# RetNet retention with a leaky-ReLU feed-forward layer: the copy that begins a product's PSUM bank moved ahead of four activations, and a new order of banks and sums between the kernel's two parts

## The chip, the cores and the metric

The kernel runs on one core of a Trainium2 chip. The metric is the device time of the whole kernel in microseconds. The core's engines work side by side, each through its own queue of instructions: TensorE (PE) multiplies matrices into PSUM, an accumulator memory of 8 banks of 128 x 512 float32; VectorE (DVE) and ScalarE (ACT) read and write PSUM and the on-chip memory SBUF; GpSimd (POOL) works on SBUF; SyncE (SP) issues transfers (DMA).

## What is computed

The first part is a recurrent retention over 4 batches, 8 heads, 768 tokens and 64 dimensions, the second a feed-forward layer with a leaky ReLU over the 3072 tokens that result, with d_model 512 and d_ff 2048.

```python
for t in range(S):
    state = gamma * state + einsum('bhd,bhe->bhde', k[:, :, t], v[:, :, t])
    y[:, :, t] = scale * einsum('bhd,bhde->bhe', q[:, :, t], state)
x = y.transpose(0, 2, 1, 3).reshape(3072, 512)
h = x @ w_in
g = np.maximum(0.01 * h, h)
out = g @ w_out
```

## The kernel before

The tokens are cut into six chunks of C = 128 per batch, so a chunk `c` is 4 x 128 = 512 token columns. The retention of a chunk is done as scores within the chunk, a mask, products with the values, and a state carried to the next chunk. d_ff is cut into four units `u` of 512. For each pair (c, u) the kernel makes a hidden product (x by w_in), the leaky ReLU, and an output product (g by w_out) that is summed into `o` over the four units and then stored.

Every such product of 2 x 2 blocks is done by a scheme with seven block products, M1 to M7, in place of eight, at the price of additions on VectorE and ScalarE. In `seven` (L515) the seven products share four PSUM banks, called A, B, C and D, and `takes` (L626 for `output`) is called after each with what has to be read out of the bank. `output` (L608) yields after each of the seven, so its caller decides with `products(steps, n)` (L1086) how many are issued before other work. In the order FUSED (L510) they come as M1, M5, M6, M2, M7, M3, M4. M7 ends the sum in bank B; `takes` copies B to bank D on ScalarE (L646) and adds B to o[3] on VectorE, and M4, the last, adds to what was copied into D. So M4 can't begin before that copy is done. The copy by which M1 begins bank B is at L628.

The kernel has two parts. The first treats chunks 0 and 1 and brings the weights into a form that is kept in DRAM (`kept`). Its steps are driven by generators, with other work hung onto their steps in tables (`hidden_more`, `output_more` near L925: an entry `s3=[...]` is done after the generator's step 3). At its end, output (0, 3) carries the visit of chunk 2 (`visit`, the last products of its retention), the loads of the next heads (`next_heads`), the differences of x (`differ`) and the sums of x in two groups (`sums_of_x`, L954, eight VectorE instructions for group 0 and four for group 1).

The PSUM pools of the first part are then closed (L981), and one pool of eight banks is opened. The second part treats chunks 2 to 5, in 16 steps `n` = (c, u). There each hidden product is itself done with seven products at two levels: `inner` (L1027) does the seven products of the inner level for four (group 0) or three (group 1) outer products at once, in bank[0:4], evacuated by ScalarE copies (L1040 to L1048) into `made`; the L1040 copy begins bank 3, to which the inner M6 adds. `outer` (L1060) sums the results into `g` on VectorE: two additions after group 0, five after group 1, and with group 1 the four leaky ReLUs on ScalarE (L1070). The output products use bank 5, 4, 7 and 6 as A, B, C and D (`room`, L1097). `fill` (L1091) is a matmul that does nothing but mark a bank as written, so that later products add to what an engine has copied there. In the steps with u = 0 or 1 of the second part's first three chunks, a `joint_visit` does the retention of the next chunk for two batches.

The order of the work is written out by hand: each engine executes its instructions in the order in which the program issues them (`manual_schedule`), and semaphores are set by the framework where one instruction needs another's data or bank. In the loop over n (L1122) the order of issue is: differences of g(n); inner and outer of step n + 1, group 0; a visit in the steps with u = 0 or 1; M1, M5, M6, M2 of output n; inner and outer of n + 1, group 1; M7, M3, M4 of output n:

```python
        products(steps, 4)
        ...
        if more:
            inner(n + 1, 1)
            outer(n + 1, 1)
        ...
        products(steps, 3)
```

## Time and profile before

The time is 720.31 us, the median of two runs (719.93 and 720.69). The profiled execution spans 717.0 us.

| engine | busy us | share of span | instructions |
|---|---|---|---|
| PE, matmuls | 665.6 | 93% | 5583 |
| PEld, weight loads | 590.7 | 82% | 5583 |
| DVE | 473.0 | 66% | 782 |
| ACT | 265.1 | 37% | 495 |
| POOL | 23.2 | 3% | 45 |

In lines of the profile, "L536" is the line of the kernel at which an instruction was issued; where a helper issues many, all have the helper's line. L536 is the products of `seven`, L1036 those of `inner`, L480 and L483 all additions and subtractions, L569 the fill, L156 the scores. A line of a timeline gives the start, the duration, the engine, what is written and read, how many instructions are merged (x16), and in brackets the engine's idle time before and what ended it. A block product of `seven` is 8 matmul instructions, since it has two column blocks, two depths and two passes for float32. The mean TensorE clock that was granted over the run is 0.963 of full speed; a table of windows gives it for each stretch.

### The profile page before, as it was taken

The numbers are of one execution on the slowest core, as the hardware profiler recorded it, in microseconds if no ns is written. First come the engines' busy times: TensorE is split into PE (matmuls) and PEld (weight loads), VectorE is DVE, ScalarE is ACT, GpSimd is POOL, SyncE is SP. The second block draws the span as 40 slices with busy tenths as digits, with TensorE's granted clock in tenths as the row PEclk, the third lists the DMA queues.
The fourth block names the chain that finished last, engine by engine and source line by source line (L and its number), as shares of the span: only waits on it lengthen the run. The fifth ranks groups of instructions, "written<-read, shape, count | busy, mean of one in ns | idle before, by whom it ended". The sixth has DMA issues, their size and how long they took to land.

```text
span 717.0 us, 13274 instructions
## 1 busy us (share of the span) xinstructions
PE 665.6 (93%) x5583; PEld 590.7 (82%) x5583; DVE 473.0 (66%) x782; ACT 265.1 (37%) x495; POOL 23.2 (3%) x45
## 2 busy tenths in 40 slices
PE   8999999999996999888898988989989889889887
PEld 5888888888885889778798887988888779779876
DVE  5889698798798474556657457575645665644663
ACT  5855664472530142313333323243242333343330
POOL 1000000000111001010000101000010000000000
PEclk9999999999999899999999999999999999999998
DMA  9922345557665866343535545325623353453201
GB/s 338 388 72 62 115 151 175 172 159 243 257 220 167 297 209 223 116 182 90 168 118 159 213 139 204 108 78 186 215 78 104 89 169 118 125 176 104 77 1 60
DMA packets 87533, 113.36 MB, mean 158 GB/s; under 512 B 3240, under 2 KB 71720, under 8 KB 87472
## 3 DMA queue, kind: packets, MB, share of 16 engines
q1 hardware_dynamic: 87312, 111.95, 47.1%
q8 instruction: 44, 0.72, 0.4%
q10 hardware_dynamic: 160, 0.55, 0.2%
q14 instruction: 17, 0.14, 0.1%
HBM read 93.35 MB, written 19.14 MB: 157 GB/s over the span
## 4 chain that ended last, share of the span: by engine, by line
PE 78%; DVE 14%; ACT 4%; DMA 2%; issue 2%; DVEq 0%
PE bank L1036 25%; PE bank L536 24%; DVE g L480 4%; DVE made L480 3%; PE A_o L536 3%; PE C_h L536 3%; PE B_h L536 3%; ACT g L1070 3%; PE B_o L536 2%; PE A_h L536 2%; PE C_o L536 2%; PE d L557 2%; PE D_o L536 2%; PE D_h L536 1%; DMA wa<-kept 1%
## 5 line engine op out<-in xcount | busy, mean ns | idle before, releaser
L480 DVE TENSOR_TENSOR made<-made,bank 128x512 f32<-128x512 f32 (+1 forms) x96 | 56.8, 619 | 104.2 <-PE bank L1036 101.3
L480 DVE TENSOR_TENSOR o<-o,bank 128x512 f32<-128x512 f32 (+2 forms) x91 | 58.7, 662 | 83.6 <-PE bank L536 65.3
L536 PE MATMUL bank<-gd,w 128*128 128x256 f32 x288 | 79.2, 431 | 26.3 <-ACT bank L646 25.6
L536 PEld LDWEIGHTS bank<-gd,w 128*128 128x128 f32 x288 | 59.7, 211 | 40.6 <-ACT bank L646 30.4
L536 PE MATMUL bank<-g,w 128*128 128x256 f32 x384 | 91.0, 386 | 0.3 <-DVE x L269 0.3
L536 PEld LDWEIGHTS bank<-g,w 128*128 128x128 f32 x384 | 72.2, 193 | 10.2 <-DVE x L269 0.5
L1036 PEld LDWEIGHTS bank<-x,wb 128*128 128x128 f32 x672 | 77.6, 192 | 1.4
L1036 PE MATMUL bank<-x,wb 128*128 128x128 f32 x672 | 77.6, 275 | 0.0
L1036 PE MATMUL bank<-x,wa 128*128 128x128 f32 x512 | 71.0, 282 | 0.0
L1036 PEld LDWEIGHTS bank<-x,wa 128*128 128x128 f32 x512 | 67.8, 201 | 2.5 <-ACT bank L1040 0.2
L1070 ACT ACTIVATE g<-g 128x512 f32<-128x512 f32 x64 | 39.4, 630 | 54.6 <-DVE g L480 54.6
L1036 PE MATMUL bank<-t,wa 128*128 128x128 f32 x384 | 57.4, 289 | 0.9 <-DMA wa<-kept 0.9
L1040 ACT COPY bank<-bank 128x512 f32<-128x512 f32 (+1 forms) x32 | 16.5, 517 | 109.6 <-PE bank L1036 109.5
L1036 PEld LDWEIGHTS bank<-t,wa 128*128 128x128 f32 x384 | 52.5, 207 | 1.1 <-DMA wa<-kept 1.1
L628 ACT COPY bank<-bank 128x512 f32<-128x512 f32 x17 | 9.7, 570 | 108.6 <-PE bank L536 92.3
L480 DVE TENSOR_TENSOR g<-made 128x512 f32<-128x512 f32 x64 | 42.9, 690 | 2.8
L483 DVE TENSOR_TENSOR gd<-g,gd 128x512 f32<-128x512 f32 x48 | 33.2, 692 | 3.0
L536 PE MATMUL bank<-gd,last 128*128 128x256 f32 (+1 forms) x124 | 29.1, 389 | 6.4 <-ACT bank L646 6.4
L536 PEld LDWEIGHTS bank<-gd,last 128*128 128x128 f32 x124 | 23.4, 197 | 10.8 <-ACT bank L646 7.6
L536 PE MATMUL bank<-g,last 128*128 128x256 f32 x120 | 30.5, 403 | 0.0
L536 PEld LDWEIGHTS bank<-g,last 128*128 128x128 f32 x120 | 24.2, 206 | 3.9 <-issue 0.3
L536 PE MATMUL A_h<-x,w 128*128 128x256 f32 x112 | 26.6, 380 | 0.0
(182 smaller groups left out, 1021.4 us busy)
## 6 DMA issues: line engine op xcount, KB each, us to landing
wa<-kept SPq DMA_DIRECT2D x16, 1344.0 KB, 7.2
raw<-in_weights_dram SPq DMA_DIRECT2D x31, 512.0 KB, 4.5
wb<-kept SPq DMA_DIRECT2D x16, 896.0 KB, 5.3
kv<-in_kv_dram SPq DMA_DIRECT2D x15, 512.0 KB, 8.1
wa<-kept SPq DMA_DIRECT2D x16, 448.0 KB, 4.1
wb<-kept SPq DMA_DIRECT2D x16, 448.0 KB, 6.3
out_dram<-o SPq DMA_DIRECT2D x23, 256.0 KB, 2.1
kept<-w SPq DMA_DIRECT2D x12, 448.0 KB, 5.6
```

The lines of the kernel that those rows point to most:

```text
L480: nc.vector.tensor_tensor(out=out, in0=a, in1=b, op=ALU.add)
L483: nc.vector.tensor_tensor(out=out, in0=a, in1=b, op=ALU.subtract)
L536: nc.tensor.matmul(to, lhsT=block(w, sa)[:, k, ts(i, 128)], rhs=rhs[:, k, a:z], start=(first and (i == 0 or split) and n == 0 and k == 0), ...
L557: nc.tensor.matmul(banks[r][:, i, :], lhsT=block(2 * u, r + 2 * kh)[:, k, ts(i, 128)], rhs=x[:, 2 * kh + th, k, :], start=(step == 0 and i ...
L628: nc.scalar.copy(out=bank_of("B"), in_=ps)
L1036: nc.tensor.matmul(ps[q][:, i], lhsT=w[:, j, i], rhs=part_of(moving[i], s), start=(i == 0 and m in ("M1", "M5", "M4")), stop=True, skip_gr ...
L1040: nc.scalar.copy(out=ps[3], in_=ps[0])
L1070: nc.scalar.activation(g[:, i], g[:, i], AF.Prelu, alpha=0.01)
```

## The change

Four edits, none of which adds or removes an instruction.

1. In the loop over n, one call `products(steps, 1)` is put between `inner(n + 1, 1)` and `outer(n + 1, 1)`. It issues M7 there, with the copy of B to D and the add of B to o[3]; so the copy stands ahead of the four leaky ReLUs in ScalarE's queue, and the add ahead of five additions in VectorE's. TensorE's order is the same, as the last call then finds only M3 and M4 to issue. In the prologue of the second part, M4 of the output product of chunk 1 is likewise issued ahead of `outer(0, 1)`.
2. The list of eight banks is rotated by four: the inner products and scores use the banks that the first part's feed-forward products used, the output products those of its retention.
3. The differences of chunk 2's x are made after step 3 of output (0, 3), ahead of the next loads, and no longer after step 4.
4. The sums of x for group 0 come after step 6 (the last products) of output (0, 3), and no longer after step 5; those for group 1 come in the second part, after five products of the output of chunk 1.

They are for the waits at two places: for M4 behind the leaky ReLUs, and for the first writes to banks where the two parts meet.

```diff
@@ -939,7 +939,7 @@
         (0, 3): dict(s0=[scored(2, 0), scored(2, 1)], s2=[lambda: visit(2, 0)],
-                     s3=[next_heads], s4=[differ(2)], s5=[sums(2, 0)], s6=[sums(2, 1)]),
+                     s3=[differ(2), next_heads], s6=[sums(2, 0)]),
     }
@@ -981,6 +981,7 @@
     bank = [banks.tile([128, 4 * C], FP32, name=f"bank{i}") for i in range(8)]
+    bank = bank[4:] + bank[:4]
@@ -1111,13 +1112,14 @@
     products(last, 2)
+    sums_of_x(2, 1)
     fill(3)
     inner(0, 0)
     outer(0, 0)
     products(last, 1)
     inner(0, 1)
+    products(last, 1)
     outer(0, 1)
-    products(last, 1)
@@ -1147,6 +1149,7 @@
         if more:
             inner(n + 1, 1)
+            products(steps, 1)
             outer(n + 1, 1)
```

## The prediction

> **What bounds the kernel now.** I read the page first: PE is busy 93% of the span and makes 78% of the chain that ended last, DVE 66%, ACT 37%. So the span is PE's work plus PE's gaps plus what a slower PE clock costs. The waits of PE say who makes the gaps:

> ```profile
> engine line waited for: us in total, times, longest us
> PE bank L536 <- ACT bank L646: 32.0, 15, 2.1
> PE bank L569 <- DVE o L480: 6.3, 1, 6.3
> PE bank L156 <- issue: 3.2, 2, 2.7
> ```

> The first row is the copy that begins bank D for M4, the second the first write to the new banks where the two parts meet. All other rows together are under 9 us. The timeline of one step (n with u = 3) shows how the first arises:

> ```profile
> 350.10 3.62 PE L536 MATMUL bank<-g,w 128*128 128x256 f32 x16
> ...
> 351.42 0.69 DVE L480 TENSOR_TENSOR g<-made 128x512 f32<-128x512 f32 x1
> ...
> 352.15 1.23 ACT L1070 ACTIVATE g<-g 128x512 f32<-128x512 f32 x2 [2.71 <-DVE g L480]
> ...
> 354.08 1.23 ACT L1070 ACTIVATE g<-g 128x512 f32<-128x512 f32 x2 [0.70 <-DVE g L480]
> 355.22 0.58 ACT L646 COPY bank<-bank 128x512 f32<-128x512 f32 x1
> 355.83 1.28 DVE L480 TENSOR_TENSOR o<-o,bank 128x512 f32<-128x512 f32 x2 [1.18 <-ACT bank L646]
> ...
> 355.85 2.59 PE L536 MATMUL bank<-gd,w 128*128 128x256 f32 x8 [2.13 <-ACT bank L646]
> ```

> The 16 instructions at 350.10 are M7 and M3. M7 is done near 352.0, but its copy (L646) stands behind four leaky ReLUs that themselves wait for VectorE, and starts at 355.22. M4 waits for it. M4 then takes 2.59 us for 8 instructions. Windows of 2 us across this step, with the granted clock third from the end, tell why:

> ```profile
> 356.00:358.00 2.00, 2.00 (x8) 1.70 (x9) 1.12 (x2) 0.00 (x0) 0.00 (x0) 0.78 0.14 38
> 358.00:360.00 2.00, 2.00 (x11) 1.91 (x10) 1.48 (x3) 0.00 (x0) 0.00 (x0) 0.50 0.00 0
> 360.00:362.00 2.00, 2.00 (x17) 2.00 (x17) 1.97 (x4) 1.16 (x2) 0.00 (x0) 0.87 0.00 0
> 386.00:388.00 2.00, 2.00 (x21) 2.00 (x19) 1.93 (x4) 1.37 (x3) 0.00 (x0) 1.00 0.35 131
> ```

> After the gap the clock is halved for a while: the first three windows lose (0.22 + 0.50 + 0.13) x 2 = 1.70 us of PE work. The last is the step after, whose gap was as long but was not followed by a halving. The transition shows in the timeline too:

> ```profile
> 225.59 1.89 PE L536 MATMUL B_o<-g,last 128*128 128x256 f32 x8
> ...
> 227.84 0.68 DVE L480 TENSOR_TENSOR o<-o,C_o 128x512 f32<-128x512 f32 x1
> ...
> 232.48 1.28 DVE L480 TENSOR_TENSOR o<-o,B_o 128x512 f32<-128x512 f32 x2
> ...
> 233.82 1.03 PE L569 MATMUL bank<-mask 128*128 128x512 bf16 x2 [6.34 <-DVE o L480]
> ...
> 234.65 3.37 PE L536 MATMUL bank<-g,last 128*128 128x256 f32 x8
> ```

> PE stops after B_o until VectorE has added B_o to o, and VectorE makes eight sums of x2 between C_o and B_o.

> [...]

> **The copy ahead of the leaky ReLUs.** No instruction is added or removed, so the cost is order alone. Take T = 350.10, the start of M7. PE instructions of 256 columns follow each other at (3.62 - 0.38) / 15 = 0.216 us, so M7 and M3 would let M4 start at T + 16 x 0.216 = T + 3.45; it started at T + 5.75. That is 2.30 us (the row says 2.13, as the modelled end of M3 overlaps). After: M7's last result is there at T + 1.89, the copy runs T + 1.93 to T + 2.51 (0.58 us; ScalarE's last evacuation of the inner products ended at T - 0.66), nearly 1 us before M4 needs it. The wait goes: 15 x 2.30 = 34.5 us.

> The halved clock: summing clock loss over 2 us windows from 226 on gives 25.9 us, of which 3.4 lie around the transition, 1.7 after the issue gap of 2.7 us at 306, 0.2 behind the last matmul. The rest, 20.5 us, follows 12 of the 15 waits (12 x 1.71). In the first 200 us, where gaps were short, the clock read 1.00 throughout. I take it that all 20.5 us come back; the other end is none.

> What the edit pushes back: the add of bank B to o[3] now stands on VectorE ahead of outer(n, 1). It waits for the copy (T + 2.55), and so the five adds of outer begin at T + 3.15 in place of T + 1.32, 1.83 us later, and so do the leaky ReLUs: they end near T + 7.0. Behind them on ScalarE stands L1040, the copy that begins bank 3 for the next inner product's M6: T + 7.0 to T + 7.55. PE would begin that inner at T + 24 x 0.216 = T + 5.18, and M6 after 24 instructions of (3.07 - 0.275) / 25 = 0.112 us, at T + 7.87. So it fits by 0.3 us. In the steps with u = 0 the copy of D to o[2] (0.58 us) lies between: L1040 ends at T + 8.1, 0.3 us too late, in four steps about 1 us together. VectorE then has o[1], o[2] and four differences, ending near T + 10.6; it is wanted at T + 5.18 + 5.63 = T + 10.8 by the inner's own adds, and the next M1 and M5 at T + 11.4 and later find g and gd ready. In a step with u = 3 four more sums (2.2 us) make those adds late, to T + 15, but nobody needs the banks before the next inner group, another 32 product instructions (6.9 us) after T + 11.4. Cost nothing.

> **The transition.** The fill still waits for VectorE: in the changed program its first weight load waits for the second add of B_o, though its bank is now one of the others; so I put the other banks themselves at nothing. What helps is that VectorE comes there sooner. From D_o at 223.00 it has four differences (about 2.8 us, plus about 0.5 beside the GpSimd decay, as the 1.20 us of one shows), A_o, C_o and B_o twice at 0.6 to 0.7: end near 229.5 in place of 233.8. So 4.3 us of the gap go and about 2.2 stay, and a gap of this length halved the clock 12 times in 15: loss expected 1.4 us, against some 1.9 before (fills 0.4 late, 24 instructions in 6.75 in place of 5.2). Gain 4.8, between 4.3 and 6.2. The eight sums move behind, to 229.5 to 233.5, before the first inner (old 246.68, new near 242) needs them; group 1's four sums lie behind M7's add, near 243, and are needed in inner(0, 1), 8 us later. The loads of wa are issued behind the stores of o, at about 230, and land after 8.3 us (median to landing in this stretch), 238: in time. In the first step M4's add now precedes outer, which delays the leaky ReLUs and L1040 by up to 1 us: 1 us lost.

> **Sum.** 34.5 + 20.5 + 4.8 - 1 - 1 = 57.8 us, so 720.3 - 57.8 = 662.5 us.

> **Rivals.**
> - *The gap goes, the slow clock stays.* [...]20.5 us are kept: 683.0; with half of the episodes, 672.8. For: 2.13 us sufficed, and the gap of 2.7 us at 306 comes from instruction issue, which this edit doesn't touch. Against: the first 200 us have small gaps and no loss, and visits without a wait before them read 1.00.
> - *ScalarE or VectorE becomes the wait.* The margin at L1040 is 0.3 us. If each of seven dependent operations comes 0.1 us later, PE loses 0.4 us in each of 15 steps: 668.5; if it is 1.5 us, 685. For: the four leaky ReLUs and L1040 follow without a gap. Against: every duration above is from this trace.
> - *It ends slower.* If the lengthened chain returned in full, with the old stall moved to M6 and 1.83 us added in every step, 15 x 1.83 - 4.8 = +22.7, 743. For: the add now ahead is real work on the chain. Against: M4 and half an inner product, 4.4 us of PE work, lie in between.

> **How the numbers follow.** Forecast 0.66; slow clock in part or whole 0.15; ScalarE or VectorE 0.17; slower 0.02. The range 655 to 677 holds the forecast, with a transition better by 1.4 and the 0.3 to 2 us of the small terms, lost issue gaps with their halving (2.7 + 1.7) at the low end, half of the clock loss or 1 us per step of new wait at the high end. Faster by over 2% (below 705.9) covers all but the last rival: 0.97, same 0.02, slower 0.01.

> **What would show it.** Right: the row of waits on L646 is gone or under 1 us; clock 0.99 or 1.00 from 250 on; M4's 8 instructions last 1.9 us; the fill's wait is near 2 us; L1040 shows no PE wait over 0.3 us. Wrong: a new row of PE waiting for L1040 or for g, or windows of 0.50 in the visits.

## Result, and the profile after

The changed kernel takes 658.87 us (658.36 and 659.38), against 720.31 before. The ratio is 0.9147, with a 95% interval from 0.9108 to 0.9186. The forecast was 662.5 us, with a range from 655 to 677.

The waits of PE, of the kernel after (what waits, for whom; total us, times, longest):

```profile
engine line waited for: us in total, times, longest us
PE bank L156 <- issue: 3.1, 2, 2.7
PE bank L569 <- DVE o L480: 2.0, 1, 2.0
PE C_h L536 <- DVE o L480: 1.7, 2, 0.8
PE bank L1037 <- DMA wa<-kept: 1.2, 1, 1.2
...
PE bank L1037 <- ACT bank L1041: 0.9, 1, 0.9
```

The row of 15 waits on L646 is gone, and the fill waits 2.0 us in place of 6.3. One row is new: PE waits 0.9 us, once, for L1041, the copy that was L1040 before. PE is now busy 98% of the span and 89% of the chain that ended last. The timeline of a step with u = 3, the one that the prediction used:

```profile
337.55 3.62 PE L536 MATMUL bank<-g,w 128*128 128x256 f32 x16
...
339.48 0.57 ACT L646 COPY bank<-bank 128x512 f32<-128x512 f32 x1 [2.59 <-PE bank L536]
340.08 0.69 DVE L480 TENSOR_TENSOR o<-o,bank 128x512 f32<-128x512 f32 x1 [1.31 <-ACT bank L646]
340.69 0.68 DVE L480 TENSOR_TENSOR g<-made 128x512 f32<-128x512 f32 x1
...
341.01 1.89 PE L536 MATMUL bank<-gd,w 128*128 128x256 f32 x8
...
343.33 1.23 ACT L1071 ACTIVATE g<-g 128x512 f32<-128x512 f32 x2 [0.70 <-DVE g L480]
...
344.47 0.58 ACT L1041 COPY bank<-bank 128x512 f32<-128x512 f32 x1
```

With T = 337.55 the copy starts at T + 1.93 and M4 at T + 3.46, without a bracket behind it. L1041 follows the leaky ReLUs at T + 6.92. M4 takes 1.89 us for its 8 instructions, in place of 2.59, since the clock no longer drops to 0.50 behind a gap. The window in which M4 runs (granted clock third from the end):

```profile
340.00:342.00 2.00, 2.00 (x11) 1.77 (x10) 1.92 (x4) 0.64 (x2) 0.00 (x0) 1.00 1.07 371
```

Where the parts meet:

```profile
226.06 1.89 PE L536 MATMUL B_o<-g,last 128*128 128x256 f32 x8
...
228.04 0.68 DVE L480 TENSOR_TENSOR o<-o,C_o 128x512 f32<-128x512 f32 x1
...
228.63 1.27 DVE L480 TENSOR_TENSOR o<-o,B_o 128x512 f32<-128x512 f32 x2
...
229.97 0.60 PE L569 MATMUL bank<-mask 128*128 128x512 bf16 x2 [2.02 <-DVE o L480]
...
230.41 1.89 PE L536 MATMUL bank<-g,last 128*128 128x256 f32 x8
```

The sums no longer stand between C_o and B_o; the fill follows B_o's last add at once, and the products behind it run at full clock (1.89 us where it was 3.37).

The difference of the two profiled spans is 717.0 - 657.7 = 59.3 us. It adds up: 15 gaps of 2.30 us are 34.5; the clock loss behind them was 20.5; from the start of B_o to the first inner product the time fell from 246.68 - 225.59 = 21.09 to 240.96 - 226.06 = 14.90, which is 6.2; the new wait for L1041 takes 0.9, and four inner products last 0.27 us longer, 1.1. That is 34.5 + 20.5 + 6.2 - 0.9 - 1.1 = 59.2 us.

### The profile page after: what moved, and what is told of

Read it like the earlier page. It is cut to its first block, busy times and chain, and to the rows that moved or that the text cites. A ratio compares the mean times of both kernels' runs of the same rounds, so it can differ in the third digit from the quotient of the medians.

```text
span 657.7 us, 13289 instructions
## 1 busy us (share of the span) xinstructions
PE 641.3 (98%) x5583; PEld 575.6 (88%) x5583; DVE 468.9 (71%) x782; ACT 263.6 (40%) x495; POOL 23.7 (4%) x45
## 4 chain that ended last, share of the span: by engine, by line
PE 89%; DVE 7%; issue 2%; ACT 1%; DMA 1%; DVEq 0%
PE bank L536 31%; PE bank L1037 26%; PE C_h L536 3%; PE A_o L536 3%; PE B_h L536 3%; PE B_o L536 3%; PE A_h L536 3%; PE C_o L536 3%; PE d L557 2%; PE D_o L536 2%; PE D_h L536 2%; PE bank L156 1%; PE bank L224 1%; DVE o L480 1%; PE bank L189 1%
## 5 line engine op out<-in xcount | busy, mean ns | idle before, releaser
L480 DVE TENSOR_TENSOR made<-made,bank 128x512 f32<-128x512 f32 (+1 forms) x96 | 56.4, 618 | 72.5 <-PE bank L1037 67.7
L480 DVE TENSOR_TENSOR o<-o,bank 128x512 f32<-128x512 f32 (+2 forms) x91 | 58.6, 661 | 59.7 <-PE bank L536 38.4
L536 PE MATMUL bank<-g,w 128*128 128x256 f32 x384 | 90.7, 385 | 0.3 <-DVE x L269 0.3
L536 PEld LDWEIGHTS bank<-g,w 128*128 128x128 f32 x384 | 72.0, 193 | 10.2 <-DVE x L269 0.5
L1037 PE MATMUL bank<-x,wa 128*128 128x128 f32 x512 | 68.9, 276 | 1.0 <-ACT bank L1041 0.9
L536 PE MATMUL bank<-gd,w 128*128 128x256 f32 x288 | 66.3, 379 | 0.8 <-issue 0.8
L1037 PEld LDWEIGHTS bank<-x,wa 128*128 128x128 f32 x512 | 63.9, 192 | 2.8 <-ACT bank L1041 1.9
L536 PEld LDWEIGHTS bank<-gd,w 128*128 128x128 f32 x288 | 54.6, 190 | 8.6 <-issue 1.2
L1037 PE MATMUL bank<-t,wa 128*128 128x128 f32 x384 | 53.4, 275 | 1.2 <-DMA wa<-kept 1.2
L1037 PEld LDWEIGHTS bank<-t,wa 128*128 128x128 f32 x384 | 48.0, 192 | 1.4 <-DMA wa<-kept 1.4
L628 ACT COPY bank<-bank 128x512 f32<-128x512 f32 x17 | 9.7, 570 | 96.7 <-PE bank L536 71.4
L480 DVE TENSOR_TENSOR g<-made 128x512 f32<-128x512 f32 x64 | 42.7, 688 | 1.1
L1041 ACT COPY bank<-bank 128x512 f32<-128x512 f32 (+1 forms) x32 | 16.7, 522 | 64.9 <-PE bank L1037 64.8
L536 PE MATMUL bank<-g,last 128*128 128x256 f32 x120 | 28.1, 380 | 0.0
L646 ACT COPY bank<-bank 128x512 f32<-128x512 f32 x16 | 9.1, 570 | 46.8 <-PE bank L536 46.8
L536 PE MATMUL bank<-gd,last 128*128 128x256 f32 (+1 forms) x124 | 27.5, 373 | 0.0
L536 PE MATMUL A_h<-x,w 128*128 128x256 f32 x112 | 26.6, 380 | 0.0
L536 PEld LDWEIGHTS bank<-gd,last 128*128 128x128 f32 x124 | 22.8, 190 | 3.2 <-DVE gd L483 0.3
```

The lines of the kernel that those rows point to most:

```text
L480: nc.vector.tensor_tensor(out=out, in0=a, in1=b, op=ALU.add)
L536: nc.tensor.matmul(to, lhsT=block(w, sa)[:, k, ts(i, 128)], rhs=rhs[:, k, a:z], start=(first and (i == 0 or split) and n == 0 and k == 0), ...
L628: nc.scalar.copy(out=bank_of("B"), in_=ps)
L646: nc.scalar.copy(out=bank_of("D"), in_=ps)
L1037: nc.tensor.matmul(ps[q][:, i], lhsT=w[:, j, i], rhs=part_of(moving[i], s), start=(i == 0 and m in ("M1", "M5", "M4")), stop=True, skip_gr ...
L1041: nc.scalar.copy(out=ps[3], in_=ps[0])
```

## Experiments

The theory: the gap in front of M4 and the halved clock behind it were two separate losses with one cause, the place of the copy in ScalarE's queue; the order of VectorE's sums gave the rest. The rivals: the clock falls for another reason, the rotation of the banks does the work where the parts meet, or most came from there.

### The loop edit alone

```diff
 (kernel before)
             inner(n + 1, 1)
+            products(steps, 1)
             outer(n + 1, 1)
```

> The kernel before with the loop edit alone (M7 and its copy issued ahead of the leaky ReLUs), banks and order of sums where the parts meet as before. Theory (the gap and the halved clock behind it go, the transition stays): 720.3 - 34.5 - 20.5 = 665.3 us; the row of waits on L646 gone, the 6.3 us wait of the fill kept, clock 1.00 after 250 us but for one issue gap. Rival (the slow clock stays): 683 or more. Rival (most of the 61 us came from where the parts meet): above 690.

Measured: 665.27 us (before, in the same rounds, 719.67), ratio 0.9248 (0.9212 to 0.9285). The first two rows of its waits of PE:

```profile
PE bank L569 <- DVE o L480: 6.5, 1, 6.5
PE bank L156 <- issue: 3.9, 2, 3.4
```

No row for L646 is left, the fill's wait is, and behind it the clock is halved as in the kernel before (0.50 from 232 to 236 us). Both rivals fall: this one line brings 54 of the 61 us.

### The rest without the loop edit

```diff
 (changed kernel)
             inner(n + 1, 1)
-            products(steps, 1)
             outer(n + 1, 1)
```

> The changed kernel with the loop edit taken back: other banks, other order of sums and M4 ahead of outer in the prologue are kept. Theory (these are worth the 6.2 us by which the first inner product comes sooner after B_o, less about 1 us for the first step): 715 us, 15 waits of 2.1 us on L646 and about 12 halvings kept. Rival (the two halves help each other): further from 715 than 2 us, in either direction.

Measured: 714.43 us, ratio 0.9928 (0.9902 to 0.9954), so 5.2 us less than before, with an interval that stays clear of 1. Its waits of PE:

```profile
PE bank L536 <- ACT bank L646: 32.0, 15, 2.1
...
PE bank L569 <- DVE o L480: 2.0, 1, 2.0
```

Counting stretches of halved clock in windows of 2 us, 12 of the 15 gaps are again followed by one, though two of the three steps that are spared are others than in the kernel before. The two halves of the change add: 54.4 + 5.2 = 59.6, against 61.4 for both.

### The gap kept, but filled

```diff
 (kernel before)
-        products(steps, 3)
+        products(steps, 2)
+        for _ in range(10 if more else 0):
+            fill(0)
+        products(steps, 1)
```

The fills are matmuls of a mask into bank 0, which has been read out by then; nothing reads them. M4 waits for its copy as before.

> The kernel before with ten bf16 fill matmuls of 512 columns (10 x 0.216 = 2.2 us) into bank 0 between M3 and M4 in 15 steps: M4 still waits for its copy at the same time, but the array is not idle. It does extra work that nothing reads. Theory (the halved clock comes from the idle gap): all 15 gaps of 2.3 us kept, 20.5 us of clock loss gone: 700 us. Rival (the clock falls for another reason, such as low activity in the stretch): 720 us or more.

Measured: 696.14 us, ratio 0.968 (0.9639 to 0.9721). One step of it, in the timeline, and the window behind it:

```profile
343.21 3.62 PE L536 MATMUL bank<-g,w 128*128 128x256 f32 x16
...
346.66 2.32 PE L569 MATMUL bank<-mask 128*128 128x512 bf16 x10
...
348.32 0.58 ACT L646 COPY bank<-bank 128x512 f32<-128x512 f32 x1
...
348.96 1.99 PE L536 MATMUL bank<-gd,w 128*128 128x256 f32 x8
```

```profile
350.00:352.00 2.00, 2.00 (x16) 1.90 (x15) 1.24 (x3) 0.12 (x1) 0.00 (x0) 1.00 0.00 0
```

M4 starts at T + 5.75, exactly as in the kernel before, and 150 more matmuls were executed, yet the kernel is 23.5 us faster. The sum of clock loss from 200 us to the last matmul is 3.4 us, all of it where the parts meet; the kernel before has 25.6. Of these 22.2 us, 20.5 are the twelve halvings behind M4's waits, of which none is left, and 1.7 the one behind the issue gap, which was short in this execution. Most of the other 1.9 us between the spans (717.0 to 692.9) is that shorter issue gap. So the halved clock behind M4 comes from PE's idle time (12 of 15 waits were followed by one with 2.13 us idle, none with that time filled), and costs what it was put at. The gap itself is the rest: the spans of this kernel and of the loop edit alone differ by 692.9 - 663.9 = 29.0 us. The loop edit's profile has 3.9 us more of issue gaps and a halving behind one of them (1.7 us), which makes 34.6, where 34.5 were counted for the gaps.

### Less of the gap filled

The same with `range(5 ...)` and `range(2 ...)`.

> As the kernel with ten fills in the gap, with five (1.1 us): some 1.2 us of each gap stay idle, M4 starts as before. Theory ([...]1.2 us are too few): no halvings behind the 15 gaps, 696 us as with ten fills. Rival ([...]): 12 halvings, 717 us; between the two if only some do.

> The same with two fills (0.4 us): some 1.9 us of each gap stay idle. Theory (the edge lies near 2 us): some of the 15 gaps are followed by a halving, fewer than 12: 700 to 714 us. Rival (the edge is sharp and above 1.9 us): 696 us. Rival (sharp and below): 717 us.

Measured: 698.76 us (0.9718; 0.9693 to 0.9742) with five, 702.16 us (0.9761; 0.9733 to 0.9788) with two. The row of M4's wait in each:

```profile
PE bank L536 <- ACT bank L646: 15.8, 15, 1.1
```

```profile
PE bank L536 <- ACT bank L646: 25.5, 15, 1.7
```

With 1.05 us idle per step no halving follows any of the 15, as expected. With 1.7 us idle none of the 15 is followed by one either. There the expectation missed: it looked for a halving behind some of them, and the clock fits its rival of an edge above what is left idle, 1.7 us as measured. That the time came to lie within the expected 700 to 714 us is chance. By the profiles, the time that both have over the 696 us with ten fills is no loss of these steps. With two, the spans differ by 701.4 - 692.9 = 8.5 us: issue gaps of 5.7 us in place of 1.4, and 3.4 us of clock loss behind one of them, where the kernel with ten fills has none. With five they differ by 4.5 us: issue gaps of 5.3 us, and a wait of the fill of 6.5 us in place of 5.4.

### The copy after two of the four leaky ReLUs

```diff
 (kernel before; outer gets a parameter `between`)
         plus(to(1), to(1), m3)
         leaky(1)
+        if between is not None:
+            between()
...
-            outer(n + 1, 1)
+            outer(n + 1, 1, lambda: products(steps, 1))
```

> The kernel before with M7 and its copy issued after the first two of the four leaky ReLUs (loop only). The two leaky ReLUs end at T + 3.3 us, the copy at T + 3.8, M4 could start at T + 3.45: a gap of about 0.4 us per step. Theory (a short gap costs its length and no halving): 665.3 + 15 x 0.4 = 671 us, clock 1.00. Rival ([...]): up to 690 us, windows of 0.50 behind most steps.

Measured: 671.4 us, ratio 0.9326 (0.928 to 0.9371). Its timeline:

```profile
320.01 3.62 PE L536 MATMUL bank<-g,w 128*128 128x256 f32 x16
...
322.06 1.23 ACT L1070 ACTIVATE g<-g 128x512 f32<-128x512 f32 x2 [2.71 <-DVE g L480]
323.20 0.58 ACT L646 COPY bank<-bank 128x512 f32<-128x512 f32 x1
...
323.83 1.99 PE L536 MATMUL bank<-gd,w 128*128 128x256 f32 x8 [0.20 <-ACT bank L646]
```

M4 starts at T + 3.82 in place of T + 3.46, a gap of 0.36 us: 15 x 0.36 = 5.4 us, of the 6.1 us by which this kernel is slower than the loop edit alone. Only the gap is paid: no halving follows any of the 15, whose idle stretches are 0.20 us. Half the move brings most of the gain (48.3 of the 54.4 us of the loop edit), because the tail of the queue, not its head, had been in the way.

### What was pushed back: the add on VectorE

```diff
 (changed kernel)
                     nc.scalar.copy(out=bank_of("D"), in_=ps)
+                if held is not None:
+                    held.append(lambda: (add(3, ps), store(3)))
+                    return
...
             products(steps, 1)
             outer(n + 1, 1)
+            for do in held:
+                do()
```

This one and the next two ran beside the changed kernel itself:

> The changed kernel itself, on the chip and in the rounds of the three next to it. Theory: 659 us, as its first runs.

Measured: 661.11 us, ratio 0.9205 (0.9163 to 0.9248); 2 us more than in its first runs, at a ratio whose interval overlaps.

> The changed kernel, but the add of bank B to o[3] on VectorE is issued behind outer, only the copy ahead of it. Theory (the add pushes outer, the leaky ReLUs and the copy at L1041 back by 1.8 us, which costs some 0.3 us in each of the four steps with u = 0): 1 us less than the changed kernel, 658 us; the 26 instructions of the inner product in those steps last 3.07 us and no longer 3.34; the first step, whose order is that of the changed kernel, keeps its 0.9 us. Rival (order on VectorE is free): same as the changed kernel. Rival (the late add holds up the differences of g): slower by 1 us or more.

Measured: 659.08 us, ratio 0.9185 (0.9147 to 0.9224). The intervals overlap, so the times alone don't tell them apart. The timelines do. PE in one step with u = 0, of the changed kernel:

```profile
287.35 3.34 PE L1037 MATMUL bank<-x,wa 128*128 128x128 f32 x26
```

and of this one:

```profile
287.26 3.07 PE L1040 MATMUL bank<-x,wa 128*128 128x128 f32 x26
```

The changed kernel has 3.34 us in the four steps with u = 0, this one has 3.07 in all. Its one wait for the copy that begins bank 3, in the first step, is kept (1.5 us). So the add ahead costs 1.1 us by the timelines, as forecast, and the late add holds up nothing.

### The rotation of the banks alone

```diff
 (changed kernel)
-    bank = bank[4:] + bank[:4]
```

> The changed kernel without the rotation of the banks. Theory (the fill waits for VectorE's last add of B_o whichever bank it writes, so the rotation is worth nothing): same as the changed kernel within 0.5 us, the fill's wait 2.0 us. Rival (the rotation is what shortened the wait): up to 4 us slower.

Measured: 661.01 us, ratio 0.9207 (0.9165 to 0.9248); the changed kernel beside it took 661.11. Its timeline where the parts meet:

```profile
229.57 1.27 DVE L480 TENSOR_TENSOR o<-o,B_o 128x512 f32<-128x512 f32 x2
230.90 0.11 PEld L569 LDWEIGHTS <-mask 128*128 128x128 bf16 x2 [2.42 <-DVE o L480]
230.91 0.61 PE L569 MATMUL bank<-mask 128*128 128x512 bf16 x2 [2.02 <-DVE o L480]
```

The wait is the same 2.02 us. The rotation is worth nothing; what shortens the wait is the order of VectorE's differences and sums (edits 3 and 4, which no run took apart).

### A version beyond the change

To the kernel with the add behind outer:

```diff
-                     s3=[differ(2), next_heads], s6=[sums(2, 0)]),
+                     s3=[next_heads], s6=[differ(2), sums(2, 0)]),
...
     inner(0, 1)
-    products(last, 1)
     outer(0, 1)
+    products(last, 1)
```

> As the kernel with the add behind outer; further, the differences of chunk 2 are made after the last product of output (0, 3), ahead of the sums, and M4 of chunk 1's output is issued behind outer(0, 1) again. Theory (VectorE reaches B_o's last add at 229.2 and not at 229.9, so the fill's wait is 1.3 us and not 2.0; the first step's wait of 0.9 us for L1041 goes): 1.5 us less than the kernel with the add behind outer, 656.5 us. Rival (the later differences and sums hold up the masks and with them the fill of bank 7 and the first inner product): a new wait there, no gain.

Measured: 656.7 us, ratio 0.915 (0.9106 to 0.9193), 2.4 us less than its neighbour by the medians, though the intervals overlap. The timeline shows what was meant:

```profile
226.33 1.89 PE L536 MATMUL B_o<-g,last 128*128 128x256 f32 x8
226.53 0.69 DVE L480 TENSOR_TENSOR o<-o,C_o 128x512 f32<-128x512 f32 x1 [1.04 <-PE C_o L536]
...
228.26 1.28 DVE L480 TENSOR_TENSOR o<-o,B_o 128x512 f32<-128x512 f32 x2 [1.04 <-PE B_o L536]
...
229.60 0.60 PE L569 MATMUL bank<-mask 128*128 128x512 bf16 x2 [1.38 <-DVE o L480]
```

VectorE now waits for PE and not the reverse; the 1.38 us that stay are the two adds of B_o themselves. No wait for the masks or the sums came instead, and that for the copy of bank 3 fell from 1.5 to 0.2 us; the two waits make 1.9 us of the gain. Run again beside the next kernel:

> The kernel with the add behind outer and the differences later, again, beside the next one. Theory: 656.7 us as before, with one issue gap of 2.7 us and a halving behind it.

Measured: 655.68 us, ratio 0.9119 (0.9097 to 0.9142).

### The issue gap, and the loads

The largest wait left is an issue gap in the second visit (2.65 us in the kernel of the section before), and the clock halves behind it in 11 of the 14 profiles. There the transfer engines read fully busy (1.07 and 1.08 in the two windows from 294 to 298 us).

```diff
 (kernel of the section before, in joint_visit)
-        for i in range(2):
-            ahead(c + 1, b + i)
-        for at in later:
-            load_kv(*at)
-        for at in later:
-            decay_v(*at)
+        def rest():
+            ...
+        return rest
 (and in the loop)
         if visiting:
             fill(3)
+            rest()
```

> The same, but the loads that a visit issues (q and k of the visit after next, k and v of the next) and the decay of v are issued after four products and no longer inside the visit, so that they don't stand in flight together with the load of wa. Theory ([...]): the gap falls below 1 us, clock 1.00, about 4 us less than its neighbour, 652.5 us. Rival (the gap has nothing to do with the transfers): same as its neighbour. Rival (later loads come late for the next visit): slower.

Measured: 656.73 us, ratio 0.9132 (0.9108 to 0.9156), no faster than its neighbour. PE in that visit:

```profile
295.87 1.40 PE L156 MATMUL bank<-qk 64*64 64x128 f32 x55
300.08 0.44 PE L156 MATMUL bank<-qk 64*64 64x64 f32 x9 [2.81 <-issue]
300.45 1.99 PE L538 MATMUL bank<-g,w 128*128 128x256 f32 x8
```

The gap stays at 2.8 us; that it waits for these transfers was my estimate, and was not shown. It isn't a full test of the transfers: the load of wa was still in flight, and they read 1.04 to 1.11 busy from 294 to 300. In this execution no halving followed.

## Why the prediction was right

- *The gap, 34.5 us.* Right. M4 starts at T + 3.46 (forecast T + 3.45), the copy at T + 1.93 (the same). The copy after two leaky ReLUs shows the gap as a length that can be dosed.
- *The halved clock, 20.5 us.* Right. From 226 us on the kernel after loses 1.7 us of clock, all behind the issue gap. That it follows from idle time, not from the stretch of the program, is shown by the filled gap: all twelve halvings gone with M4's start unchanged at T + 5.75.
- *What is pushed back, 2 us.* Right. L1041 starts at T + 6.92, forecast T + 7.0; steps with u = 0 lose 0.27 us, forecast 0.3; the first step 0.9, forecast up to 1.
- *Where the parts meet, 4.8 us.* The mechanism was right, the term too small: 6.2 us, its upper end. VectorE's last add of B_o ended near 229.9 (forecast 229.5, and the whole stretch came 0.47 us later), the wait was 2.02 us (forecast 2.2). The mis-sized term is the clock: I put 1.4 us of expected loss behind this gap, taking the 12 in 15 of the 2.13 us gaps for it, and none came. Five profiles have this wait of 2.0 us, and in none a halving follows it. In that of the changed kernel it falls in two parts, 0.88 and 1.14 us, into two of the stretches of 3.41 us that the last section comes to.
- *The rest.* 57.8 forecast and 1.4 more here make the 59.2 of the profiles. The medians differ by 61.4, since the profiled run before was 1.6 us faster than its median (718.76 and 720.31) and the one after 0.5 slower; that is run to run.
- *The rivals.* No small gap in the visits was followed by a halved clock: the one halving that is left stands behind the 2.7 us issue gap. ScalarE became the wait in 2 us of the whole. Nothing came back in M6 beyond that.

## What to carry to other kernels

A wait of the bounding engine can cost twice: its own length, and a slower clock behind it (34.5 and 20.5 us here); add up the clock loss by windows before sizing an edit. To be rid of the second cost, a gap need only get shorter, not vanish (12 halvings behind 15 gaps of 2.13 us here, none behind 15 of 1.7). In a queue that runs in order, as ScalarE's does here (the copy began at T + 5.12 behind the leaky ReLUs and at T + 1.93 ahead of them), put what the bounding engine waits for ahead of work that itself still waits, and look whether what it pushes back has a wait of its own within that margin (0.27 us in the steps with u = 0). Where a first write waits for a whole region to be read out, the order of the reader's queue matters, and which bank is written first may not (a wait of 2.02 us with either order of the banks).

## What was not expected

- *Gaps of nearly one length differ in what follows.* Idle stretches of PE of 0.2, 1.05 and 1.7 us in front of M4 (15 each) were followed by no halving, those of 2.13 us by 12 of 15, in both kernels that have them. Where the parts meet, 2.0 us were followed by none in five profiles, 5.4 to 6.5 us by one in six of six. In front of M4 the edge lies between 1.7 and 2.13 us. Length alone doesn't decide, though: three of 15 gaps of 2.13 us were spared, and so were three issue gaps of 2.5 to 2.8 (two with five fills, one with the later loads).
- *The halvings lie on a grid of their own.* M4 in the last four steps of the kernel before:

```profile
616.12 3.43 PE L536 MATMUL bank<-gd,last 128*128 128x256 f32 x8 [2.13 <-ACT bank L646]
643.23 3.23 PE L536 MATMUL bank<-gd,w 128*128 128x256 f32 x8 [2.13 <-ACT bank L646]
670.33 3.03 PE L536 MATMUL bank<-gd,w 128*128 128x256 f32 x8 [2.13 <-ACT bank L646]
697.42 2.82 PE L536 MATMUL bank<-gd,w 128*128 128x256 f32 x8 [2.13 <-ACT bank L646]
```

The two traces can be cut into these stretches of 3.41 us, with PE's idle time summed in each, from 6 us after the start to the last matmul. In the kernel before, 14 at full clock had 2.12 us of idle or more, and each was followed by a halved one; the 177 others had 1.93 us or less, and none was. In the changed kernel one had 2.48 us and was followed by a halved one; the 187 others had 1.13 us or less, and none was. A gap across the border of two stretches is shared between them. First a gap that was followed by a halving and one that was spared, in the kernel before, then the issue gap of 2.81 us with the later loads. The second number is the stretch's length, the third the time in which PE was busy:

```profile
353.69:357.11 3.42, 1.29 (x7) 1.13 (x7) 2.24 (x4) 1.72 (x3) 0.00 (x0) 1.00 0.79 233
357.11:360.52 3.41, 3.41 (x15) 3.15 (x14) 1.99 (x4) 0.33 (x1) 0.00 (x0) 0.50 0.02 5
...
381.00:384.41 3.41, 1.48 (x7) 1.32 (x8) 2.02 (x4) 1.72 (x3) 0.00 (x0) 1.00 0.73 198
```

```profile
294.96:298.37 3.41, 2.31 (x103) 2.01 (x100) 2.75 (x9) 0.00 (x0) 0.00 (x0) 1.00 1.07 373
298.37:301.78 3.41, 1.70 (x15) 1.41 (x15) 1.73 (x5) 0.00 (x0) 0.00 (x0) 1.00 1.04 405
301.78:305.20 3.42, 3.42 (x18) 3.01 (x17) 1.18 (x3) 0.57 (x1) 0.41 (x1) 1.00 0.63 248
```

PE is idle for 2.13 us in the first stretch, and the next one is halved. In the spared step 1.93 us of the gap fall into one stretch; of the 2.81 us, 1.10 fall into one and 1.71 into the next. In the other two spared steps of the kernel before it is 1.90 and 1.43 us, so all three lie below the 2.12. No run set a gap's place on the grid on purpose, and the ends of matmuls are modelled, so these figures hold for idle time as the profiler shows it.
- *A few useless matmuls can pay.* Two fills, which cut the idle stretch in front of M4 from 2.13 to 1.70 us, were enough: no halving in 15 steps, and 702.16 us where the kernel before took 718.99.
- *The issue gap sits at a fixed count of PE's instructions.* In the visit it comes with 9 of 64 score matmuls left. With 2, 5 and 10 fills added ahead of it, it came with 11, 14 and 19 left:

```profile
309.09 0.52 PE L156 MATMUL bank<-qk 64*64 64x64 f32 x9 [2.74 <-issue]
```

```profile
308.48 0.90 PE L156 MATMUL bank<-qk 64*64 64x64 f32 x11 [2.53 <-issue]
```

```profile
305.27 0.66 PE L156 MATMUL bank<-qk 64*64 64x64 f32 x19 [0.49 <-issue]
```

These are the kernel before and those with two and ten fills. A place that moves so is one in the stream of instructions, and not in the data. Counted in the traces of the kernel before and of the changed one, 5569 of PE's instructions lie ahead of it in both, and the issue gaps that follow (0.44 and 0.75 us, and 0.40 and 0.82) come 1280 and then 768 instructions on: 5 and 3 times 256. The gap in the visit lasted 2.4 to 3.4 us in 13 of 14 profiles and 0.49 us in the last line; what sets its length stays open.
